# LayerNorm statistics in bf16, V behind Q in the first pair, fewer warm-up matmuls, and b2 added on VectorE, in a one-core transformer block

## The chip, the cores and the metric

The kernel runs on one core of a Trainium2 chip. The metric is the device time of one execution in microseconds; lower is better. The engines are named as in the profile: PE (TensorE matmuls), PEld (its weight loads), DVE (VectorE), ACT (ScalarE), POOL (GpSimd), and SP, which issues the DMAs.

## The reference

One transformer block over x of 1 x 2048 x 1024 in bf16, with 32 heads of 32:

```python
h  = x + (softmax(q k^T / sqrt(32)) v) @ wo       # q, k, v = layernorm(x) @ wqkv, per head
h2 = h + gelu(layernorm(h) @ w1 + b1) @ w2 + b2   # w1 1024 x 3584, gelu by tanh
```

layernorm subtracts the mean and divides by sqrt(variance + 1e-5), with no gain and no offset. All the inputs and the output are bf16.

## The kernel before

**Tiling.** The 2048 rows are 16 tiles of 128 or 8 chunks of 256. The 32 heads are 8 groups g of 4 heads (128 columns). A *round* (`Job.round`) is the scores of one g, one chunk of queries and 256 keys: eight matmuls with K = 32, four side by side in the array (line 705), two Exp of 128 x 1024 on ACT (713), an addition on DVE for the softmax sum (720), eight matmuls of P times V (725), and four with a column of ones for the sum (744). There are 8 x 8 x 8 = 512 rounds, so 1024 Exp. Scores lie in three pairs of PSUM banks and a round uses two pairs, so the scores of a round wait for the first Exp of the round before.

**Stages.** In the *lead*, the x tiles come two by two (eight pairs): LayerNorm on DVE (`layer_norm`), transposition (`tr_tile`, on PE for the first two pairs, by DMA for the others), the projections K, Q and V of the first heads, and the first 16 rounds. The statistics of the second x tile are taken by ACT (554). Then come the other groups' projections with the attention of chunks 0 and 1, and after that, per chunk c, attention(c) with work of the chunks before put between: the output projection `wo(c-1)`, `ln2(c-1)`, `ffn2(c-2)` and `ffn1(c-1)`. In the *tail*, after the last Exp, come wo(7), ln2(7), what is left of ffn2(6), ffn1(7) and ffn2(7). ffn2 of a chunk is four *groups* (two tiles of rows by two halves of the columns) of 28 accumulating matmuls of 512 columns. Ahead of them in a group stands a matmul that puts 2 x b2 into PSUM, from `two_row` (a matrix with 2.0 in row 0) and `b2t` (b2 in row 0, zeros below; 867). DVE then writes 0.5 x PSUM + h (875). The tail's ffn2(7) has no such matmul: there b2 is loaded on all partitions into `b2b` (1025) and added to h in f32 (`hb`, 1027).

**Order.** The program's order on each engine is worked out when the kernel is built. Every piece of work is a task with a cost in microseconds, a priority and dependencies; `Graph.schedule` plays them through, and `pick_pe` chooses PE's next one: scores first when they are ready, then PV, then the *background* (projections, wo, ffn), then warm-up matmuls (`kind="warm"`) if there is nothing else. The costs that matter here are 0.930 and 0.915 for the two Exp of a round (`EXP`, 473), 0.2165 for a 512-column background matmul (`mm`), 0.217 for a round's scores, and 0.108 for a change of PE's tiling mode (`switch`, 112). On the chip each engine then runs its list strictly in that order, with semaphores between engines. Background matmuls go as four column tiles of 32 (502) or, in ffn1, the lead and the tail, as one full matmul (505).

**LayerNorm** (545 to 581): `bn_stats` twice and `bn_aggr` per tile give mean and variance in f32 (`mv`). A copy rounds them to bf16 (`mvb`, 570), an addition puts eps on the variance (571), POOL takes the root (573), a copy turns the mean into f32 (575), and a reciprocal (576) and the normalisation (578) follow.

**Warm-up** (903): 80 matmuls of 256 columns that read `ident` and `b2t`. They wait for POOL's setting of both; the memset of `b2t` is POOL's last (540).

```python
    EXP = (0.930, 0.915)
...
        proj_k(group("lead", FULL), 0, 256 * i, 256, "act")
        if i < 2:
            proj_q(group("lead", FULL), 0, 256 * i, 256, i, "dve")
        proj_v(group("lead", FULL), 2 * i, 0, "act")
```

Of the kernel before, what the change touches and what calls it, by code (L numbers as in the profile page):

```python
# [8 lines left out]
ALU = mybir.AluOpType  # L9
# [3 lines left out]
P = 128  # L13
BF = dt.bfloat16
# [298 lines left out]
def build_kernel(nc, A_x, A_wqkv, A_wo, B_w1, B_b1, B_w2, B_b2, out):  # L313
# [45 lines left out]
    top = Area(BASE)  # L359
    ident, B_ident = sb(top, "ident", [P, P], BF)  # L360
    ones32, B_ones = sb(top, "ones32", [P, 32], BF)
    two_row, B_two = sb(top, "two_row", [P, P], BF)
    b2t, B_b2t = sb(top, "b2t", [P, D], BF)
    b1b, B_b1b = sb(top, "b1b", [FC, P], BF)
    b1f, B_b1f = sb(top, "b1f", [P, FC], F32)
    cexp, B_cexp = sb(top, "cexp", [P, 16], F32)
    NLN = 8
    st_l, B_stl = sb(top, "st", [P, NLN, 12], F32, NLN)
    mv_l, B_mv = sb(top, "mv", [P, NLN, 2], F32, NLN)
    mvb, B_mvb = sb(top, "mvb", [P, NLN, 2], BF, NLN)  # L370
    mvr, B_mvr = sb(top, "mvr", [P, NLN, 1], F32, NLN)
    tb, B_tb = sb(top, "tb", [P, NLN, 1], BF, NLN)
    denb, B_denb = sb(top, "denb", [P, NLN, 1], BF, NLN)
# [106 lines left out]
    def group(name, full=False):  # L480
        g = Group((1, len(groups)), gr.buf())
        g.full = full
        g.name = name
        groups.append(g)
        return g

    def grp_pe(g, fns, occ, reads, mode):
        t = pe(fns, occ, reads=reads, writes=[g.buf], mode=mode)
        t.grp = g
        return t  # L490

# [36 lines left out]
    def dma_t(out_ap, in_ap, reads, writes, prio=0):  # L528
# [3 lines left out]
    pool(lambda g: g.affine_select(out=ident[:], in_=ident[:], compare_op=ALU.not_equal, fill=1.0,  # L532
                                   base=0, pattern=[[-1, P]], channel_multiplier=1), 0.4,
         reads=[B_ident], writes=[B_ident])
    pool(lambda g: g.memset(cexp[:, 0:8], 0.5), 0.2, writes=[B_cexp])
    pool(lambda g: g.memset(cexp[:, 8:16], -1.0), 0.2, reads=[B_cexp], writes=[B_cexp])
    pool(lambda g: g.memset(ones32[:], 1.0), 0.2, writes=[B_ones])
    pool(lambda g: g.memset(two_row[:], 0.0), 0.3, writes=[B_two])
    pool(lambda g: g.memset(two_row[0:1, :], 2.0), 0.3, reads=[B_two], writes=[B_two])
    pool(lambda g: g.memset(b2t[:], 0.0), 1.0, writes=[B_b2t])  # L540

    cnt = {"ln": 0}
    LEAD_PRIO = -4
# [1 line left out]
    def layer_norm(tiles, prio, on_act=(), after=()):  # L545
        n = len(tiles)
        while cnt["ln"] % NLN + n > NLN:
            cnt["ln"] += 1
        i = cnt["ln"] % NLN
        cnt["ln"] += n  # L550
        for k, (x_ap, B_x, o_ap, B_o) in enumerate(tiles):
            if k in on_act:
                for f, fn in enumerate((ACT.Copy, ACT.Square)):
                    act(lambda a, k=k, x_ap=x_ap, f=f, fn=fn: a.activation(
                        junk, x_ap, fn, scale=1.0, accum_out=st_l[:, i + k, f:f + 1]), 1024 + 112,
                        reads=B_x, writes=[B_stl[i + k], B_junk], prio=-1)
                dve(lambda v, k=k: v.tensor_scalar(mv_l[:, i + k, 0:1], st_l[:, i + k, 0:1], 1.0 / D, None, ALU.mult), 0.12,
                    reads=[B_stl[i + k]], writes=[B_mv[i + k]], prio=prio)
                dve(lambda v, k=k: v.scalar_tensor_tensor(st_l[:, i + k, 2:3], mv_l[:, i + k, 0:1], -1.0, mv_l[:, i + k, 0:1], ALU.mult, ALU.mult),
                    0.12, reads=[B_mv[i + k]], writes=[B_stl[i + k]], prio=prio)  # L560
                dve(lambda v, k=k: v.scalar_tensor_tensor(mv_l[:, i + k, 1:2], st_l[:, i + k, 1:2], 1.0 / D, st_l[:, i + k, 2:3], ALU.mult, ALU.add),
                    0.12, reads=[B_stl[i + k]], writes=[B_mv[i + k]], prio=prio)
                continue
            for c in range(2):
                dve(lambda v, c=c, k=k, x_ap=x_ap: v.bn_stats(st_l[:, i + k, 6 * c:6 * c + 6], x_ap[:, 512 * c:512 * c + 512]),
                    0.68, reads=[B_x[c % len(B_x)]], writes=[B_stl[i + k]], prio=prio, after=after)
            dve(lambda v, k=k: v.bn_aggr(mv_l[:, i + k, :], st_l[:, i + k, :]), 0.2,
                reads=[B_stl[i + k]], writes=[B_mv[i + k]], prio=prio)
        sl = slice(i, i + n)
        dve(lambda v: v.tensor_copy(mvb[:, sl, :], mv_l[:, sl, :]), 0.12, reads=B_mv[sl], writes=B_mvb[sl], prio=prio)  # L570
        dve(lambda v: v.tensor_scalar(tb[:, sl, :], mvb[:, sl, 1:2], EPS_BF, None, ALU.add), 0.12,
            reads=B_mvb[sl], writes=B_tb[sl], prio=prio)
        pool(lambda g: g.tensor_tensor(denb[:, sl, 0], tb[:, sl, 0], cexp[:, 0:n], ALU.pow), 0.42 + 0.157 * n,
             reads=B_tb[sl] + [B_cexp], writes=B_denb[sl], prio=prio)
        dve(lambda v: v.tensor_copy(mvr[:, sl, :], mvb[:, sl, 0:1]), 0.12, reads=B_mvb[sl], writes=B_mvr[sl], prio=prio)
        dve(lambda v: v.reciprocal(rden[:, sl, :], denb[:, sl, :]), 0.12, reads=B_denb[sl], writes=B_rden[sl], prio=prio)
        for k, (x_ap, B_x, o_ap, B_o) in enumerate(tiles):
            t = dve(lambda e, k=k, x_ap=x_ap, o_ap=o_ap: e.tensor_scalar(
                o_ap, x_ap, mvr[:, i + k, :], rden[:, i + k, :], ALU.subtract, ALU.mult), 0.58,
                reads=B_x + [B_mvr[i + k], B_rden[i + k]], writes=[B_o], prio=prio)  # L580
        return [t]
# [217 lines left out]
    def ln2_tile(R, c, t, evac):  # L799
        o, bo = R.xb.next()  # L800
        layer_norm([(hch[:, c % 2, t, :], B_hch[c % 2][2 * t:2 * t + 2], o, bo)], LN2_PRIO)
        if evac == "dma":
            dma_t(hnT[:, t, :, :], o, [bo], [B_hnT[t]], prio=-1)
        else:
            transposes(group(f"t{c}.{t}"), o, bo, hnT[:, t, :, :], B_hnT[t], evac)

    def ln2(R, c, evac):
        for t in range(2):
# [46 lines left out]
    def ffn2(R, c, j, t, tail=False):  # L855
# [4 lines left out]
        for h in range(512 // n):  # L860
            grp = group(f"f2.{c}.{j}{t}.{h}")
            grp.soft = {d for _, _, d in ws}
            grp.dmas = [d for _, _, d in ws]
            grp.soft |= soft[c]
            grp.gate = [gate[c]]
            if not tail:
                mm(grp, two_row[:, :], b2t[:, 512 * j:512 * j + 512], True, False, [B_two, B_b2t])
            at = slice(512 * j + n * h, 512 * j + n * h + n)
            for fc in range(FC):
                w, bw, _ = ws[fc // 4]  # L870
                mm(grp, gT[:, c % 2, fc, t * P:t * P + P], w[:, fc % 4, n * h:n * h + n], tail and fc == 0, fc == FC - 1,
                   [B_gT[c % 2][fc], bw], cols=(0, n))
            o, bo = R.os.next()
            h_ap, b_h = (hb[:, t, at], B_hb[t]) if tail else (hch[:, c % 2, t, at], B_hch[c % 2][2 * t + j])
            dve(lambda v, o=o, h_ap=h_ap, grp=grp: v.scalar_tensor_tensor(
                o[:, 0:n], psum[:, grp.bank, 0:n], 0.5, h_ap, ALU.mult, ALU.add),
                c_dve_ps(n), reads=[grp.buf, b_h], writes=[bo], prio=-2)
            dma(out2[256 * c + P * t:256 * c + P * t + P, at], o[:, 0:n], P * n * 2, reads=[bo], prio=0)
# [21 lines left out]
    load_w(WV, -6, 0, 2 * P)  # L900
    for tt in range(4, NXR):
        x_tile(tt, -6)
    for k in range(80):
        pe(lambda p: p.matmul(psum[:, 6, 0:256], ident[:, :], b2t[:, 0:256], start=True, stop=True), 0.12,  # L904
           reads=[B_ident, B_b2t], writes=[B_ps[6]], kind="warm")
# [4 lines left out]
    for i in range(8):  # L910
# [9 lines left out]
                last_x = [x_tile(tt + NXR, -4)]  # L920
        proj_k(group("lead", FULL), 0, 256 * i, 256, "act")
        if i < 2:
            proj_q(group("lead", FULL), 0, 256 * i, 256, i, "dve")
        proj_v(group("lead", FULL), 2 * i, 0, "act")
        jobs[0].round()
        if i == 1:
            jobs[1].round()
# [23 lines left out]
        rest_w(WQ + 1, c * P, c * P + P)  # L951
    rest_w(WV + 1, 256, 512)
    dma(b1b[:], B_b1.rearrange("(fc p) -> fc p", p=P), P * FC * 2, writes=[B_b1b], prio=1, after=lx)
    dma(b2t[0:1, :], B_b2.rearrange("(o d) -> o d", o=1), D * 2, writes=[B_b2t], prio=1, after=lx)

    n_lead = len(groups)
    B_ps[4].r += [t for grp in groups for t in grp.buf.r]
# [52 lines left out]
    hb, B_hb = sb(tail, "hb", [P, 2, D], F32, 2)  # L1010
    b2b, B_b2b = sb(tail, "b2b", [P, D], BF)
    slots = []
    for k in range(7):
        for lo, nm in ((kt_lo, "wk"), (v_lo, "wv")):
# [6 lines left out]
    for t in range(2):  # L1021
        for j in range(2):
            wo_group(R2, L, j, t, ws[j])
        ln2_tile(R2, L, t, "act")
    dma(b2b[:], B_b2.rearrange("(o d) -> o d", o=1).broadcast_to((P, D)), P * D * 2, writes=[B_b2b], prio=1)
    for t in range(2):
        dve(lambda v, t=t: v.tensor_tensor(hb[:, t, :], hch[:, L % 2, t, :], b2b[:], ALU.add), c_dve(1024),
            reads=B_hch[L % 2][2 * t:2 * t + 2] + [B_b2b], writes=[B_hb[t]], prio=2)
# [170 lines left out]
```

## Time and profile before

| | |
|---|---|
| median of 4 runs | 1106.34 us (1104.67 to 1106.88) |
| the profiled execution, its own time | 1106.86 us |
| its span, first to last instruction | 1105.1 us |
| PE busy | 1067.2 us (97%) |
| ACT busy | 1025.7 us (93%) |
| DVE busy | 819.5 us (74%) |
| POOL busy | 19.2 us (2%) |
| first Exp starts, last one ends | 16.19 and 1029.20 us |
| last matmul ends | 1102.49 us |

The busy share of PE comes from records whose ends are modelled and overlap, so it is read with the starts of the instructions beside it. The time of the execution is 1.8 us over its span: launch and end lie around it.

### The profile page before, as it was taken

Reading aid. Unit: us, or ns where it says so; the run is one execution under the profiler, and the core shown is the slowest. Engines: PE = TensorE matmul, PEld = TensorE weight load, DVE = VectorE, ACT = ScalarE, POOL = GpSimd, SP = SyncE. Lnnn points to the kernel's source line nnn. Section 1 sums busy time; section 2 is a strip of 40 time slices with the busy share of each in tenths; the row PEclk is TensorE's granted clock in tenths of the full one; section 3 lists DMA queues with packets and bytes.
Section 4 is the critical chain, followed back from the end, with each engine's and each line's share of the span. In section 5 each row is a group of like instructions: output and inputs, shape, how many; then the busy total and the mean of one; then the engine's idle time right before and its main releaser. Section 6 shows DMA issues by size and latency. Waiting matters only on the chain.

```text
span 1105.1 us, 42019 instructions
## 1 busy us (share of the span) xinstructions
PE 1067.2 (97%) x19196; PEld 595.0 (54%) x19196; DVE 819.5 (74%) x1461; ACT 1025.7 (93%) x1135; POOL 19.2 (2%) x37
## 2 busy tenths in 40 slices
PE   8999999999999989999999999999999999999999
PEld 6645555554444655554554455455545544554585
DVE  7456666666767888888888688878887887787563
ACT  5889999999999999999999999999999999999351
POOL 1100000000000000000000000000000000000000
PEclk9999999999999989999999999999999999999999
DMA  6960100012432854676847755764767377968770
GB/s 190 194 172 2 41 2 3 3 41 88 104 107 88 222 131 126 187 237 141 248 119 245 192 167 174 210 207 124 246 138 245 101 230 195 282 167 266 229 238 20
DMA packets 263164, 169.17 MB, mean 153 GB/s; under 512 B 50763, under 2 KB 260811, under 8 KB 262988
## 3 DMA queue, kind: packets, MB, share of 16 engines
q1 hardware_dynamic: 262988, 166.50, 53.4%
q8 instruction: 150, 2.46, 1.0%
q14 instruction: 26, 0.21, 0.1%
HBM read 152.31 MB, written 7.34 MB: 144 GB/s over the span
## 4 chain that ended last, share of the span: by engine, by line
ACT 55%; PE 43%; DVE 1%; issue 0%; POOL 0%; DVEq 0%; POOLq 0%
ACT PT L713 52%; PE ps L505 16%; PE ps L502 13%; PE ps L705 6%; PE ps L725 4%; ACT a_th L848 3%; PE ps L744 2%; PE ps L904 1%; PE ps L585 0%; DVE stg L598 0%; ACT xnT L588 0%; DVE PS L720 0%; DVE DT L753 0%; ACT V L596 0%; DVE hch L790 0%
## 5 line engine op out<-in xcount | busy, mean ns | idle before, releaser
L713 ACT ACTIVATE PT<-ps 128x1024 bf16<-128x1024 f32 x1024 | 953.8, 1075 | 12.7 <-PE ps L705 11.8
L720 DVE TENSOR_TENSOR PS<-PT 128x1024 bf16<-128x1024 bf16 x495 | 333.3, 685 | 104.3 <-ACT PT L713 80.2
L705 PE MATMUL ps<-QT,KT 32*128 32x256 bf16 x4096 | 204.0, 273 | 12.9 <-ACT PT L713 11.9
L505 PE MATMUL ps<-hnT,w1r 128*128 128x256 bf16 x1632 | 208.9, 275 | 3.9 <-DVE gT L830 1.7
L502 PE MATMUL ps<-w2r,gT 128*32 128x512 bf16 x2860 | 192.9, 383 | 0.1
L725 PE MATMUL ps<-PT,V 128*32 128x256 bf16 x4096 | 184.5, 275 | 8.7 <-ACT PT L713 7.8
L505 PEld LDWEIGHTS ps<-hnT,w1r 128*128 128x128 bf16 x1632 | 146.7, 98 | 57.2 <-issue 31.0
L705 PEld LDWEIGHTS ps<-QT,KT 32*128 32x128 bf16 x4096 | 61.1, 92 | 163.6 <-ACT PT L713 124.5
L744 PE MATMUL ps<-PS,ones 128*32 128x256 bf16 x1980 | 138.5, 275 | 1.5 <-DVE PS L720 1.2
L725 PEld LDWEIGHTS ps<-PT,V 128*32 128x32 bf16 x4096 | 91.9, 96 | 71.7 <-ACT PT L713 30.4
L502 PE MATMUL ps<-xnT,Wall 128*32 128x512 bf16 x1888 | 127.0, 381 | 3.1 <-DVE stg L598 1.3
L502 PEld LDWEIGHTS ps<-w2r,gT 128*32 128x32 bf16 x2860 | 67.2, 97 | 64.9 <-issue 26.1
L830 DVE TENSOR_TENSOR gT<-ps,b1f 128x512 bf16<-128x512 f32 x98 | 67.3, 687 | 21.8 <-PE ps L505 20.8
L505 PE MATMUL ps<-Wall,xnT 128*128 128x128 bf16 (+1 forms) x896 | 69.6, 227 | 0.5 <-DVE V L598 0.3
L502 PEld LDWEIGHTS ps<-xnT,Wall 128*32 128x32 bf16 x1888 | 43.0, 96 | 46.9 <-issue 14.4
L744 PEld LDWEIGHTS ps<-PS,ones 128*32 128x32 bf16 x1980 | 52.4, 96 | 27.1 <-issue 12.1
L849 DVE SCALAR_TENSOR_TENSOR gT<-a_th,gT 128x1024 bf16<-128x1024 f32 x49 | 59.7, 1219 | 5.7 <-ACT a_th L848 5.6
L505 PEld LDWEIGHTS ps<-Wall,xnT 128*128 128x128 bf16 x896 | 54.9, 98 | 15.5 <-issue 11.1
L502 PE MATMUL ps<-w1r,OT 128*32 128x512 bf16 x896 | 62.0, 381 | 1.0 <-DVE hch L790 0.9
L846 DVE SCALAR_TENSOR_TENSOR a_sq<-a_sq,gT 128x1024 bf16<-128x1024 bf16 x49 | 59.8, 1220 | 0.7
L848 ACT ACTIVATE a_th<-a_sq 128x1024 f32<-128x1024 bf16 x49 | 54.9, 1120 | 0.0
L753 DVE STREAM_TRANSPOSE DT<-ps 128x256 f32<-128x256 f32 x64 | 28.6, 446 | 24.1 <-PE ps L744 24.0
(85 smaller groups left out, 589.8 us busy)
## 6 DMA issues: line engine op xcount, KB each, us to landing
w2r<-in_B_w_dram SPq DMA_DIRECT2D x105, 512.0 KB, 6.3
w1r<-in_B_w_dram SPq DMA_DIRECT2D x102, 512.0 KB, 4.6
w1r<-in_A_wo_dram SPq DMA_DIRECT2D x28, 512.0 KB, 3.9
wk<-in_B_w_dram SPq DMA_DIRECT2D x9, 512.0 KB, 6.3
xrb<-in_A_x_dram SPq DMA_DIRECT2D x16, 256.0 KB, 4.4
Wall<-in_A_wqkv_dram SPq DMA_DIRECT2D x16, 256.0 KB, 5.2
wv<-in_B_w_dram SPq DMA_DIRECT2D x8, 512.0 KB, 6.6
a_x<-in_A_x_dram SPq DMA_DIRECT2D x28, 128.0 KB, 2.3
```

The lines of the kernel that those rows point to most:

```text
L502: fns.append(lambda p, j=j: p.matmul(dst(32 * j, 32 * j + 32), lhsT[:, 32 * j:32 * j + 32], rhs, start=start, stop=stop, tile_position=(0, ...
L505: t.alt = [lambda p: p.matmul(dst(0, P), lhsT, rhs, start=start, stop=stop, skip_group_check=True)]
L705: fns.append(lambda p, i=i, hh=hh, r0=r0: p.matmul(psum[:, 2 * us[hh // 2] + hh % 2, 256 * i:256 * i + 256], KT[r0:r0 + 32, g, 256 * r + P ...
L713: t = act(lambda a, u=u, q=q: a.activation(PT[:, s, 2 * q:2 * q + 2, :], psum[:, 2 * u:2 * u + 2, :], ACT.Exp, bias=0.0, scale=SCALE), 102 ...
L720: dve(lambda v: v.tensor_tensor(PS[:, z, :, :], PT[:, s, :, 0:256], PT[:, s, :, 256:512], ALU.add), c_dve(1024, 2), reads=B_PT[s], writes= ...
L725: fns.append(lambda p, i=i, hh=hh: p.matmul(psum[32 * hh:32 * hh + 32, self.bank, 0:256], V[:, g, 2 * r + i, 32 * hh:32 * hh + 32], PT[:, ...
L744: fns.append(lambda p, i=i, hh=hh, src=src: p.matmul(psum[32 * hh:32 * hh + 32, self.bank, 256:512], ones32[:, :], src[:, hh, :], start=False,
L753: dve(lambda v: v.transpose(DT[f][:], psum[:, self.bank, 256:512]), c_dve_ps(256), reads=[self.buf], writes=[B_DT[f]], prio=-1)
L830: gate[c] = dve(lambda v, xh=xh, fc=fc, grp=grp: v.tensor_tensor(xh, psum[:, grp.bank, :].rearrange("p (f n) -> p f n", f=2), b1f[:, fc:fc ...
L846: dve(lambda v: v.scalar_tensor_tensor(v4(sq), v4(sq), C2, xh, ALU.add, ALU.mult), c_dve(n), reads=[b_sq] + b_xh, writes=[b_sq], prio=1)
L848: gate[c] = act(lambda a: a.activation(th, sq, ACT.Tanh, bias=0.0, scale=K2 / 2), n, reads=[b_sq], writes=[b_th], prio=-1, kind="tanh")
L849: t = dve(lambda v: v.scalar_tensor_tensor(xh, v4(th), 1.0, xh, ALU.add, ALU.mult), c_dve(n), reads=[b_th] + b_xh, writes=b_xh, prio=1)
```

## The change

It makes five edits. (1) `bn_aggr` writes mean and variance in bf16, the rounding copy goes, and the copy of the mean to f32 is put before POOL's root; for the tile whose statistics ACT takes, the mean is computed straight in f32. (2) In the first pair, V's matmuls may start only after Q's last. (3) The warm-up is 56 matmuls of 128 columns that read `ident` alone, planned at 0.1 each. (4) The matmul of 2 x b2 goes from every ffn2 group, with `two_row`, `b2t` and their memsets; b2 is loaded on all partitions near the end of the lead, and after each LayerNorm of h an addition on DVE adds it to h in place in bf16, for the tail too, whose f32 copy goes. (5) The planner's cost of the two Exp falls to 0.922 and 0.907.

```diff
-    EXP = (0.930, 0.915)
+    EXP = (0.922, 0.907)
...
-    pool(lambda g: g.memset(two_row[:], 0.0), 0.3, writes=[B_two])
-    pool(lambda g: g.memset(two_row[0:1, :], 2.0), 0.3, reads=[B_two], writes=[B_two])
-    pool(lambda g: g.memset(b2t[:], 0.0), 1.0, writes=[B_b2t])
...
-        dve(lambda v: v.tensor_copy(mvb[:, sl, :], mv_l[:, sl, :]), 0.12, reads=B_mv[sl], writes=B_mvb[sl], prio=prio)
-        dve(lambda v: v.tensor_scalar(tb[:, sl, :], mvb[:, sl, 1:2], EPS_BF, None, ALU.add), 0.12,
-            reads=B_mvb[sl], writes=B_tb[sl], prio=prio)
+        dve(lambda v: v.tensor_scalar(tb[:, sl, :], mv_l[:, sl, 1:2], EPS_BF, None, ALU.add), 0.15,
+            reads=B_mv[sl], writes=B_tb[sl], prio=prio)
+        if not on_act:
+            dve(lambda v: v.tensor_copy(mvr[:, sl, :], mv_l[:, sl, 0:1]), 0.15, reads=B_mv[sl], writes=B_mvr[sl], prio=prio)
...
+        h = hch[:, c % 2, t, :]
+        dve(lambda v: v.tensor_tensor(h, h, b2b[:], ALU.add), c_dve(1024, 2),
+            reads=[B_b2b], writes=B_hch[c % 2][2 * t:2 * t + 2], prio=2)
...
-            if not tail:
-                mm(grp, two_row[:, :], b2t[:, 512 * j:512 * j + 512], True, False, [B_two, B_b2t])
...
-    for k in range(80):
-        pe(lambda p: p.matmul(psum[:, 6, 0:256], ident[:, :], b2t[:, 0:256], start=True, stop=True), 0.12,
-           reads=[B_ident, B_b2t], writes=[B_ps[6]], kind="warm")
+    for k in range(56):
+        pe(lambda p: p.matmul(psum[:, 6, 0:P], ident[:], ident[:], start=True, stop=True), 0.1,
+           reads=[B_ident], writes=[B_ps[6]], kind="warm")
...
-            proj_q(group("lead", FULL), 0, 256 * i, 256, i, "dve")
-        proj_v(group("lead", FULL), 2 * i, 0, "act")
+            q = group("lead", FULL)
+            proj_q(q, 0, 256 * i, 256, i, "dve")
+        v = group("lead", FULL)
+        if i == 0:
+            v.after = q.buf.w
+        proj_v(v, 2 * i, 0, "act")
...
-    dma(b2t[0:1, :], B_b2.rearrange("(o d) -> o d", o=1), D * 2, writes=[B_b2t], prio=1, after=lx)
+    dma(b2b[:], B_b2.rearrange("(o d) -> o d", o=1).broadcast_to((P, D)), P * D * 2, writes=[B_b2b], prio=1, after=lx)
...
-    dma(b2b[:], B_b2.rearrange("(o d) -> o d", o=1).broadcast_to((P, D)), P * D * 2, writes=[B_b2b], prio=1)
-    for t in range(2):
-        dve(lambda v, t=t: v.tensor_tensor(hb[:, t, :], hch[:, L % 2, t, :], b2b[:], ALU.add), c_dve(1024),
-            reads=B_hch[L % 2][2 * t:2 * t + 2] + [B_b2b], writes=[B_hb[t]], prio=2)
```

More of the change, by code (lines that the diff above doesn't have):

```diff
@@ L361, in build_kernel @@
     ones32, B_ones = sb(top, "ones32", [P, 32], BF)
-    two_row, B_two = sb(top, "two_row", [P, P], BF)
-    b2t, B_b2t = sb(top, "b2t", [P, D], BF)
+    b2b, B_b2b = sb(top, "b2b", [P, D], BF)
     b1b, B_b1b = sb(top, "b1b", [FC, P], BF)
     b1f, B_b1f = sb(top, "b1f", [P, FC], F32)
-    cexp, B_cexp = sb(top, "cexp", [P, 16], F32)
+    cexp, B_cexp = sb(top, "cexp", [P, 8], F32)
     NLN = 8
     st_l, B_stl = sb(top, "st", [P, NLN, 12], F32, NLN)
-    mv_l, B_mv = sb(top, "mv", [P, NLN, 2], F32, NLN)
-    mvb, B_mvb = sb(top, "mvb", [P, NLN, 2], BF, NLN)
+    mv_l, B_mv = sb(top, "mv", [P, NLN, 2], BF, NLN)
     mvr, B_mvr = sb(top, "mvr", [P, NLN, 1], F32, NLN)
@@ L482, in group @@
         g.full = full
+        g.after = ()
         g.name = name
@@ L487, in grp_pe @@
     def grp_pe(g, fns, occ, reads, mode):
-        t = pe(fns, occ, reads=reads, writes=[g.buf], mode=mode)
+        t = pe(fns, occ, reads=reads, writes=[g.buf], mode=mode, after=g.after)
         t.grp = g
@@ L534, in build_kernel @@
          reads=[B_ident], writes=[B_ident])
-    pool(lambda g: g.memset(cexp[:, 0:8], 0.5), 0.2, writes=[B_cexp])
-    pool(lambda g: g.memset(cexp[:, 8:16], -1.0), 0.2, reads=[B_cexp], writes=[B_cexp])
+    pool(lambda g: g.memset(cexp[:], 0.5), 0.2, writes=[B_cexp])
     pool(lambda g: g.memset(ones32[:], 1.0), 0.2, writes=[B_ones])
-    pool(lambda g: g.memset(two_row[:], 0.0), 0.3, writes=[B_two])
-    pool(lambda g: g.memset(two_row[0:1, :], 2.0), 0.3, reads=[B_two], writes=[B_two])
-    pool(lambda g: g.memset(b2t[:], 0.0), 1.0, writes=[B_b2t])
     cnt = {"ln": 0}
@@ L556, in layer_norm @@
                         reads=B_x, writes=[B_stl[i + k], B_junk], prio=-1)
[L557 to L560, printed above, removed]
+                dve(lambda v, k=k: v.tensor_scalar(mvr[:, i + k, :], st_l[:, i + k, 0:1], 1.0 / D, None, ALU.mult), 0.12,
+                    reads=[B_stl[i + k]], writes=[B_mvr[i + k]], prio=prio)
+                dve(lambda v, k=k: v.scalar_tensor_tensor(st_l[:, i + k, 2:3], mvr[:, i + k, :], -1.0, mvr[:, i + k, :], ALU.mult, ALU.mult),
+                    0.12, reads=[B_mvr[i + k]], writes=[B_stl[i + k]], prio=prio)
                 dve(lambda v, k=k: v.scalar_tensor_tensor(mv_l[:, i + k, 1:2], st_l[:, i + k, 1:2], 1.0 / D, st_l[:, i + k, 2:3], ALU.mult, ALU.add),
@@ L569, in layer_norm @@
         sl = slice(i, i + n)
-        dve(lambda v: v.tensor_copy(mvb[:, sl, :], mv_l[:, sl, :]), 0.12, reads=B_mv[sl], writes=B_mvb[sl], prio=prio)
-        dve(lambda v: v.tensor_scalar(tb[:, sl, :], mvb[:, sl, 1:2], EPS_BF, None, ALU.add), 0.12,
-            reads=B_mvb[sl], writes=B_tb[sl], prio=prio)
+        dve(lambda v: v.tensor_scalar(tb[:, sl, :], mv_l[:, sl, 1:2], EPS_BF, None, ALU.add), 0.15,
+            reads=B_mv[sl], writes=B_tb[sl], prio=prio)
+        if not on_act:
+            dve(lambda v: v.tensor_copy(mvr[:, sl, :], mv_l[:, sl, 0:1]), 0.15, reads=B_mv[sl], writes=B_mvr[sl], prio=prio)
         pool(lambda g: g.tensor_tensor(denb[:, sl, 0], tb[:, sl, 0], cexp[:, 0:n], ALU.pow), 0.42 + 0.157 * n,
              reads=B_tb[sl] + [B_cexp], writes=B_denb[sl], prio=prio)
-        dve(lambda v: v.tensor_copy(mvr[:, sl, :], mvb[:, sl, 0:1]), 0.12, reads=B_mvb[sl], writes=B_mvr[sl], prio=prio)
-        dve(lambda v: v.reciprocal(rden[:, sl, :], denb[:, sl, :]), 0.12, reads=B_denb[sl], writes=B_rden[sl], prio=prio)
+        dve(lambda v: v.reciprocal(rden[:, sl, :], denb[:, sl, :]), 0.15, reads=B_denb[sl], writes=B_rden[sl], prio=prio)
         for k, (x_ap, B_x, o_ap, B_o) in enumerate(tiles):
@@ L870, in ffn2 @@
                 w, bw, _ = ws[fc // 4]
-                mm(grp, gT[:, c % 2, fc, t * P:t * P + P], w[:, fc % 4, n * h:n * h + n], tail and fc == 0, fc == FC - 1,
+                mm(grp, gT[:, c % 2, fc, t * P:t * P + P], w[:, fc % 4, n * h:n * h + n], fc == 0, fc == FC - 1,
                    [B_gT[c % 2][fc], bw], cols=(0, n))
             o, bo = R.os.next()
-            h_ap, b_h = (hb[:, t, at], B_hb[t]) if tail else (hch[:, c % 2, t, at], B_hch[c % 2][2 * t + j])
+            h_ap, b_h = hch[:, c % 2, t, at], B_hch[c % 2][2 * t + j]
             dve(lambda v, o=o, h_ap=h_ap, grp=grp: v.scalar_tensor_tensor(
@@ L1009, in build_kernel @@
     R2.os = Ring(ring(tail, "b_os", 3, 512, BF))
-    hb, B_hb = sb(tail, "hb", [P, 2, D], F32, 2)
-    b2b, B_b2b = sb(tail, "b2b", [P, D], BF)
     slots = []
```

## The prediction

> **What bounds it now.** I read the busy shares first, then the chain that ended last, then the groups by form, then windows and timeline of the stages that the change touches.
>
> ```profile
> PE 1067.2 (97%) x19196; PEld 595.0 (54%) x19196; DVE 819.5 (74%) x1461; ACT 1025.7 (93%) x1135; POOL 19.2 (2%) x37
> ACT 55%; PE 43%; DVE 1%; issue 0%; POOL 0%; DVEq 0%; POOLq 0%
> ```
>
> The chain is shared by ACT and PE, and nothing else is on it. The windows tell the stages apart (columns: length; busy us and count of PE, PEld, DVE, ACT, POOL; granted clock; DMA share; GB/s):
>
> ```profile
> 430.00:1000.00 570.00, 555.14 (x10364) 299.92 (x10360) 462.27 (x790) 568.87 (x618) 6.44 (x10) 1.00 0.66 191
> 1030.30:1102.50 72.20, 72.19 (x487) 46.23 (x483) 37.21 (x54) 20.46 (x37) 1.10 (x2) 1.00 0.56 175
> ```
>
> The second line is the tail: PE without a gap, so what it has left to do there is its length. The first is attention with background. ACT is full, but is it the bound? In the timeline's start column the second Exp of a round starts 0.904 or 0.921 us after the first (mean 0.911), while the next round's first starts on average 0.935 later, 0.904 in six cases of ten. A round therefore takes 1.846 us (570 us less 40 tanh of 0.947, over 577 Exp, gives 1.844); the planner assumed 0.930 + 0.915 = 1.845. ACT alone could do 2 x 0.904 = 1.81. On PE, scores that follow ffn or wo matmuls start a median 0.105 us after these stream out; any change of tiling mode costs that much, so PE usually comes straight from other work. So PE's list, packed to 1.845, sets the pace, and ACT's waits (0.037 a round) are too short for the table of waits. **PE is the bound from about 56 us to 1102.5**, with ACT 2% behind.
>
> **b2 on DVE.** 7 chunks x 4 groups = 28 matmuls of 2 x b2 go. The groups by form show 104 records in four column tiles (26 groups) and 2 full ones:
>
> ```profile
> L502 PE MATMUL ps<-b2t,two_row 128*32 128x512 bf16 x104 | 10.4, 388 | 0.4 <-DVE hch L790 0.3
> L505 PE MATMUL ps<-b2t,two_row 128*128 128x512 bf16 x2 | 0.8, 379 | 0.0
> L720 DVE TENSOR_TENSOR PS<-PT 128x1024 bf16<-128x1024 bf16 x495 | 333.3, 685 | 104.3 <-ACT PT L713 80.2
> L1027 DVE TENSOR_TENSOR hb<-hch,b2b 128x1024 f32<-128x1024 bf16 x2 | 2.4, 1220 | 0.0
> ```
>
> The 388 ns is one record's length, not what PE pays, since four run side by side and the next is pipelined behind. What it pays is start to start:
>
> ```profile
> 429.12 0.40 PE L502 MATMUL ps<-b2t,two_row 128*32 128x512 bf16 x4
> 429.34 1.90 PE L502 MATMUL ps<-w2r,gT 128*32 128x512 bf16 x32
> ```
>
> 0.22 here, 0.2157 as a mean over neighbours of the same form. 28 x 0.2157 = **6.0 us off PE**: 5.6 during attention (429 to 1025 us), 0.43 in the tail. No mode change goes with it. The 5.6 count only if the freed slots fill. ffn2(6) runs ahead into attention: one group of it and 15 of 28 blocks of the next are done before the tail. So work moves up from the tail.
>
> DVE gets 16 additions of 0.685 (L720's form) and loses two of 1.22. The two tail ones have PE's unbroken 72 us over them. The 14 in attention (9.6 us) lie in DVE's idle 108 of 570 us. Queued behind one on DVE are PSUM evacuations and L720's sums, for which PE waits; the lowest priority puts it where the plan has a hole. Cost 0; if that cover were gone, each would hold PE up by its length, 9.6 us. The 256 KB load of b2b is issued where the row of b2t was (67.0 us), behind the weights of wqkv and ahead of w2 blocks that land every 1.5 us (512 KB), so it pushes these back by 0.75; w2 is first used at 429. Nothing else is moved on SP, and the same load at 1028.5 goes.
>
> **The start.** From the timeline:
>
> ```profile
> 2.65 5.66 PE L904 MATMUL ps<-b2t,ident 128*128 128x256 bf16 x33 [2.65 <-POOL b2t L540]
> 5.22 0.17 DVE L570 CAST mvb<-mv 128x2 bf16<-128x2 f32 x1
> 5.42 0.16 DVE L571 TENSOR_SCALAR tb<-mvb 128x1 bf16<-128x1 bf16 x1
> ...
> 8.15 0.61 PE L585 MATMUL ps<-ident,xb 128*128 128x128 bf16 x8
> ...
> 10.45 0.61 PE L585 MATMUL ps<-ident,xb 128*128 128x128 bf16 x8
> ...
> 12.27 1.03 PE L505 MATMUL ps<-xnT,Wall 128*128 128x256 bf16 x8
> 13.13 0.82 PE L505 MATMUL ps<-Wall,xnT 128*128 128x256 bf16 x6
> 13.86 1.03 PE L505 MATMUL ps<-xnT,Wall 128*128 128x256 bf16 x8
> ```
>
> A removed copy takes 0.20 (5.22 to 5.42) out of each of the first two LayerNorms, in series: the second tile's output ends at 8.87 instead of 9.27 (8.72 + 0.55). The f32 copy of the mean ends before POOL's root does (5.64 against 6.23): nothing. The transposes could have started at 7.05 and 9.3, but began at 8.04 and 10.34 (weight loads), behind warm-ups. After, POOL has set ident at 1.45, so warming starts about 1.5; in the planner's own costs 56 x 0.1 fit ahead of the first transposes (before, 33 x 0.12 stood there, from plan time 3.0; now it starts at 0.8), so the list has all 56 first and none later. In time, 56 of half the length end near 7.1. The second transposes then start at 8.9, 1.5 before 10.45, and K with them (its weights landed at 5.7, Q's at 6.7). Six V matmuls go from between K and Q: 0.73. The first scores wait for Q's copy: 1.5 + 0.7 = **2.3 earlier** at best. The lead then loops through ACT, PE and ACT at 5.3 us a pair and should carry it; LayerNorm of the second pair, which stood behind Q's copy on DVE (to 15.28), moves too.
>
> Against it: **the clock**. Warm-ups started 0.213 apart until 6.5 us and 0.109 after, half and full speed. Now PE is sparse from 7.1 to 10.8. The windows show that sparseness alone halves the clock:
>
> ```profile
> 23.60:27.02 3.42, 1.95 (x33) 1.00 0.94 223
> 402.48:405.90 3.42, 1.04 (x28) 1.00 0.71 175
> 405.90:409.31 3.41, 3.00 (x45) 0.50 0.65 84
> 1010.06:1013.47 3.41, 2.02 (x48) 1.00 1.17 315
> 1013.47:1016.88 3.41, 3.41 (x36) 0.50 0.95 296
> ```
>
> (columns: length, PE busy, clock, DMA). Its steps fall on one grid of 3.41 us. By streaming time (256 columns in 0.109, side by side counted once) PE was used 18% and 37% ahead of the two falls, and 42% in 23.6 to 27.0, with no fall. The new start has 20 to 45% in such a stretch, by where the grid falls: about an even chance. Half speed for K and Q's 16 matmuls costs 16 x 0.104 = 1.7, leaving 0.6; two slow windows (3.4 lost) would leave a loss of 1.1. I take 1.5 earlier, between 0.6 and 2.3. *TensorE: Matmul & The Clock Gate* of the Trainium skill, in "Why this matters for your kernels", says that pauses up to about 3 us between bursts keep the clock. By it the start gains the whole 2.3. The fall at 1013 came with no pause of 1 us, so the row decides, and I keep 1.5.
>
> **The Exp cost.** 0.016 less a round changes only the order: less background between scores. 498 rounds follow the lead, so 8.0 us of background moves toward the tail. If PE sets the pace, rounds shorten by the same and nothing is lost (perhaps ACT's 0.037 waits shrink: a gain of up to 2). If ACT does, all 8.0 is added. The nearest row, 1.846 measured against 1.845 planned, says the first; since ACT's floor is close I take a fifth, +1.6.
>
> **Other.** 23 copies of DVE off the start's path go, 0.2 each, under waits; layout shifts by some 320 bytes: 0.
>
> **Sum**, from the profiled 1106.86 (span 1105.1 + 1.8; 0.5 above the median): - 6.0 - 1.5 + 1.6 = **1100.9**.
>
> **Rivals.** (a) *The start loses*: two slow windows, 1106.9 - 6.0 + 1.1 + 1.6 = 1103.5. (b) *The removal frees nothing*: background waits for something else, as at 399 to 409 (ffn1's one input buffer) and 1009 to 1013 (the last gelu); only the tail's 0.43 is left: 1106.9 - 0.4 - 1.5 + 1.6 = 1106.5. Against: such stretches are rare from 429 on. (c) *Exp, the slower side*: the rounds stay at 1.846 and all 8.0 lands in the tail: 1106.9 - 6.0 - 1.5 + 8.0 = 1107.3. It decides once over 7.5 of the 8.0 is not won back, a round above 1.845. For: ACT is 99.8% busy. Against: its starts. (d) *DVE holds PE*: + 9.6, 1110.5; against: 81% busy. (e) *Better*: Exp costs nothing, the start gains 2.3, one slow window (1.7) goes: 1106.9 - 6.0 - 2.3 - 1.7 = 1096.8.
>
> **Chances.** Forecast 0.55, (a) 0.12, (b) 0.08, (c) 0.07, (d) 0.05, (e) 0.13. 0.2% is about what this measurement can tell. Faster by more (under 1104.1): forecast, (a), (e): 0.80. Within: (b) and half of (c): 0.12. Slower: the rest, 0.08. The range leaves out (c), (d) and half of (e): 1096.8 to 1106.5.
>
> **What would show it.** First Exp at 13.9 to 15.6 instead of 16.19; K's eight matmuls 0.109 apart (0.213 if the clock fell); rounds near 1.83 and the last Exp 7 or more earlier; from the last Exp to the last matmul 72 to 77 against 73.3; no waits of PE on the additions. Wrong if rounds stay at 1.845 with a longer tail, or if a new stretch without background appears near chunk boundaries: the order is planned anew everywhere.

## The result and the profile after

The changed kernel takes **1103.48 us** (median of 44 runs, 1100.83 to 1107.03) where the kernel before, on the same chips, takes 1106.77 (65 runs, 1104.0 to 1109.36): a ratio of **0.997, 95% interval 0.9965 to 0.9976**, or 3.3 us less. The forecast was 6.0 less. The sign and the range held; about half of the forecast gain is missing, and the rest of this document is about where it went.

The profiled execution took 1104.98 us, with a span of 1103.2. It is 1.9 below the one before. Runs of one kernel vary with their mean clock, so the medians differ by more than the two profiles: of the 44, the nine at 0.995 have a median of 1101.9, the seventeen at 0.992, the profiled one among them, 1104.0. Lines in the profile after are numbered a little differently: scores 700, Exp 708, sums 715, PV 720, background matmuls 501 and 504, tanh 846, the new addition 802.

Busy shares and the engines of the chain that ended last, in the page of the changed kernel:

```profile
PE 1059.5 (96%) x19045; PEld 588.6 (53%) x19045; DVE 824.0 (75%) x1449; ACT 1022.5 (93%) x1135; POOL 20.3 (2%) x33
ACT 77%; PE 20%; DVE 1%; DMA 1%; issue 0%; POOL 0%; DVEq 0%; POOLq 0%
```

PE is busy 7.7 us less. The chain is a first hint: ACT's share went from 55% to 77%, PE's from 43% to 20%. Work was taken from PE, and the end is now tied to ACT much more.

The windows of the changed kernel (length; busy us and count of PE, PEld, DVE, ACT, POOL; granted clock; DMA share; GB/s), for a piece of the start, for attention with background, and for the tail:

```profile
11.78:15.19 3.41, 3.41 (x18) 2.31 (x16) 2.06 (x7) 0.38 (x1) 0.70 (x1) 0.50 0.46 167
...
430.00:1000.00 570.00, 555.40 (x10326) 299.64 (x10329) 471.55 (x795) 568.21 (x619) 8.42 (x10) 1.00 0.68 194
...
1027.29:1100.68 73.39, 73.35 (x492) 46.69 (x488) 36.16 (x52) 20.46 (x37) 1.54 (x2) 1.00 0.57 177
```

The first line is a stretch at half clock that the start did not have before. The second looks like the old one (555.14 PE, 568.87 ACT), but one tanh more fits in beside the same 577 Exp: a round takes 1.840 us instead of 1.846, worked out from the starts of the Exp as in the prediction. The third shows the tail: the last Exp ends at 1026.50 (2.7 earlier) and the last matmul at 1100.68 (1.8 earlier), so the tail is 74.2 instead of 73.3.

The start on PE, from the timeline of the changed kernel (start, us, engine, line, operation, tiles, count, and in brackets the idle time before it and what ended it):

```profile
1.53 4.86 PE L900 MATMUL ps<-ident 128*128 128x128 bf16 x55 [1.53 <-POOL ident L531]
7.06 0.62 PE L580 MATMUL ps<-ident,xb 128*128 128x128 bf16 x8 [0.67 <-DVE mvr L552]
7.52 0.22 PE L900 MATMUL ps<-ident 128*128 128x128 bf16 x1
9.21 0.61 PE L580 MATMUL ps<-ident,xb 128*128 128x128 bf16 x8 [1.47 <-DVE xb L573]
10.93 2.82 PE L504 MATMUL ps<-xnT,Wall 128*128 128x256 bf16 x16 [1.12 <-ACT xnT L583]
13.54 1.85 PE L504 MATMUL ps<-Wall,xnT 128*128 128x256 bf16 x8
15.32 0.40 PE L700 MATMUL ps<-QT,KT 32*128 32x256 bf16 x8
```

Warm-ups start at 1.53 and the transpositions at 7.06 and 9.21 (forecast 7.05 and 8.9). But K and Q's 16 matmuls take 2.82, and V's eight take 1.85 where six took 0.82 before: the clock fell. The first Exp starts at 15.77, only 0.4 earlier than before.

### The profile page after: what moved, and what is told of

It is laid out like the page before. It is cut to its first block, busy times and chain, and to the rows that moved or that the text cites. A ratio compares the mean times of both kernels' runs of the same rounds, so it can differ in the third digit from the quotient of the medians.

```text
span 1103.2 us, 41713 instructions
## 1 busy us (share of the span) xinstructions
PE 1059.5 (96%) x19045; PEld 588.6 (53%) x19045; DVE 824.0 (75%) x1449; ACT 1022.5 (93%) x1135; POOL 20.3 (2%) x33
## 4 chain that ended last, share of the span: by engine, by line
ACT 77%; PE 20%; DVE 1%; DMA 1%; issue 0%; POOL 0%; DVEq 0%; POOLq 0%
ACT PT L708 73%; PE ps L504 10%; PE ps L501 5%; ACT a_th L846 4%; PE ps L700 2%; PE ps L720 2%; PE ps L739 1%; DMA hnT<-xb 1%; ACT xnT L583 0%; DMA xrb<-in_A_x_dram 0%; DVE xb L573 0%; DVE stg L593 0%; PE ps L580 0%; DVE st L560 0%; DVE a_os L871 0%
## 5 line engine op out<-in xcount | busy, mean ns | idle before, releaser
L708 ACT ACTIVATE PT<-ps 128x1024 bf16<-128x1024 f32 x1024 | 952.4, 1107 | 16.3 <-PE ps L700 15.7
```

What stands on the lines that cost most here:

```text
L708: t = act(lambda a, u=u, q=q: a.activation(PT[:, s, 2 * q:2 * q + 2, :], psum[:, 2 * u:2 * u + 2, :], ACT.Exp, bias=0.0, scale=SCALE), 102 ...
```

## The experiments

Two theories. **Terms:** each edit has its own price (PE work saved, start, Exp costs), and the prices add up; one of them was mis-sized. **Order:** PE is not the bound alone, so PE time saved or added counts only partly, and what decides is whether PE has background ready; the edits need not add up, since each one makes the planner lay out all lists anew. A special case of the second is the **gelu gate**: ffn2 of a chunk may start only after the chunk's last tanh, and the VectorE steps of gelu have a low priority (1, behind LayerNorm's -2 and the sums' -1) on an engine that runs its list strictly in order. (Letters in the quoted expectations are explained in each.)

All twelve runs; each ratio is to the kernel before on the same chip, so runs are compared by their ratios. "Rounds" is the mean length of a round from 430 to 1000 us; the tail runs from the end of the last Exp to the end of the last matmul; the "gate" columns are the start of the last tanh of the fifth and of the seventh chunk; "dry" is the sum of all stretches over 2.6 us after 430 in which PE has attention but no background matmul; "half clock" is the time at 0.50 after 430.

| kernel | median us | ratio [95%] | rounds | last Exp ends | tail | gate 5 | gate 7 | dry | half clock |
|---|---|---|---|---|---|---|---|---|---|
| before | 1106.77 | 1 | 1.846 | 1029.2 | 73.3 | 805.9 | 1012.4 | 10.4 | 3.4 |
| after | 1103.48 | 0.997 [0.9965, 0.9976] | 1.840 | 1026.5 | 74.2 | 815.1 | 1012.3 | 13.3 | 3.4 |
| b2 edit alone | 1118.75 | 1.0115 [1.0099, 1.0132] | 1.854 | 1028.9 | 83.9 | 822.3 | 1029.0 | 27.2 | 23.9 |
| Exp edit alone | 1116.98 | 1.0097 [1.0082, 1.0112] | 1.841 | 1022.6 | 89.0 | 829.7 | 1036.4 | 7.9 | 13.6 |
| start edits alone | 1107.93 | 1.0017 [1.0008, 1.0026] | 1.842 | 1024.8 | 77.7 | 819.2 | 1016.2 | 8.2 | 3.4 |
| before, b2 matmuls not issued | 1107.14 | 0.9999 [0.9987, 1.0010] | 1.847 | 1029.6 | 73.2 | 805.4 | 1013.1 | 10.7 | 3.4 |
| after, 28 matmuls doubled | 1106.3 | 0.9994 [0.9984, 1.0005] | 1.849 | 1025.3 | 74.9 | 816.3 | 1012.1 | 12.7 | 0 |
| after, additions cut short | 1102.55 | 0.9962 [0.9947, 0.9977] | 1.837 | 1024.2 | 74.0 | 814.9 | 1011.2 | 13.0 | 0 |
| after, 130 warm-ups | 1102.3 | 0.9971 [0.9958, 0.9985] | 1.839 | 1023.8 | 74.2 | 814.1 | 1010.6 | 12.8 | 0 |
| b2 edit, gelu first | 1107.82 | 1.0008 [0.9998, 1.0018] | 1.850 | 1027.9 | 74.9 | 800.0 | 1015.2 | 12.6 | 3.4 |
| before, gelu first | 1107.91 | 1.0007 [0.9996, 1.0019] | 1.847 | 1025.7 | 75.6 | 808.1 | 1014.6 | 8.2 | 0 |
| Exp edit, last gelu first | 1109.89 | 1.0026 [1.0016, 1.0037] | 1.843 | 1024.3 | 79.9 | 806.8 | 1020.5 | 17.5 | 10.2 |
| after, old Exp costs | 1105.56 | 0.9987 [0.9976, 0.9998] | 1.847 | 1030.2 | 72.2 | 805.6 | 1013.7 | 17.6 | 3.4 |
| after, 130 warm-ups, Exp 0.913 | 1107.1 | 1.0009 [0.9998, 1.0021] | 1.836 | 1020.8 | 82.1 | 830.5 | 1021.6 | 14.5 | 0 |

Rounds, gates, dry, half clock and the ends are of one profiled execution each, the medians of all runs.

### One part at a time

The b2 edit alone, on the kernel before (with `b2b` loaded in place of `b2t` and the tail's copy gone):

```diff
-            if not tail:
-                mm(grp, two_row[:, :], b2t[:, 512 * j:512 * j + 512], True, False, [B_two, B_b2t])
+        h = hch[:, c % 2, t, :]
+        dve(lambda v: v.tensor_tensor(h, h, b2b[:], ALU.add), c_dve(1024, 2), ...
```

> The kernel before with edit (4) alone: no matmul of 2 x b2, b2 added to h on VectorE; warm-ups, LayerNorm, V's place and the Exp cost stay. Theory (PE sets the pace, so freed slots fill): 6.0 us faster than before, with the last Exp about where it was and the tail shorter. Rival (the freed slots stay empty): 0.4 faster. Rival (VectorE's 14 additions hold PE up): no gain or slower.

Measured: 1118.75, **12.4 slower** than the 1106.35 of the kernel before.

The Exp edit alone:

```diff
-    EXP = (0.930, 0.915)
+    EXP = (0.922, 0.907)
```

> The kernel before with edit (5) alone: planned Exp costs 0.922 and 0.907. Theory (PE sets the pace): rounds about 0.012 us shorter, tail longer by nearly as much, time 0 to 1.6 us over before. Rival (ACT sets the pace): rounds stay at 1.846 and the time rises by up to 8 us.

Measured: 1116.98, **10.6 slower**. The last Exp does end 6.6 earlier, but the tail is 15.7 longer.

The start edits alone (bf16 statistics, V behind Q, 56 warm-ups):

```diff
-    for k in range(80):
+    for k in range(56):
...
+        if i == 0:
+            v.after = q.buf.w
```

> The kernel before with edits (1) to (3) alone: statistics in bf16, V behind Q, 56 short warm-ups. The matmuls of 2 x b2 stay. Theory: first Exp 0.4 to 2.3 us earlier and the time 0.6 to 2.3 lower. Rival (the clock falls at 11.8 us, as in the profile after, and the lead's second round comes no earlier than before): 0 to 1 us slower.

Measured: 1107.93, 1.6 slower, although the first Exp started at 14.07 in the profile, 2.1 earlier. The last Exp came 4.4 earlier there, but the tail is 4.4 longer.

Alone the three cost 12.4 + 10.6 + 1.6 = 24.6; together they gain 3.3. The theory of terms in its plain form is gone: no sum of fixed prices gives both.

### What stands in the b2 edit's way

The trace of the b2 edit alone shows a long dry stretch. PE's ffn2, wo and other four-tile matmuls (line 502), in windows of 12.8, 12.4 and 12.8 us (length; PE and PEld busy; clock; DMA share; GB/s):

```profile
795.00:807.80 12.80, 8.61 (x128) 2.81 (x120) 1.00 0.57 153
807.80:820.20 12.40, 0.04 (x4) 0.00 (x0) 0.65 0.73 128
820.20:833.00 12.80, 5.48 (x88) 1.98 (x88) 0.80 0.23 69
```

For 12.4 us there is none but the last four records of a group at the edge (and none of line 505 either), and the clock halves. Why, its timeline tells, first on VectorE, then on ACT:

```profile
802.66 1.22 DVE L849 SCALAR_TENSOR_TENSOR a_sq<-a_sq,gT 128x1024 bf16<-128x1024 bf16 x1
...
805.39 0.69 DVE L565 BATCH_NORM_STATS2 st<-hch 128x6 f32<-128x512 bf16 x1
...
808.74 0.69 DVE L565 BATCH_NORM_STATS2 st<-hch 128x6 f32<-128x512 bf16 x1
...
815.85 0.55 DVE L578 TENSOR_SCALAR xb<-hch,mvr,rden 128x1024 bf16<-128x1024 bf16 x1 [1.24 <-DMA hnT<-xb]
...
816.92 1.22 DVE L852 SCALAR_TENSOR_TENSOR gT<-a_th,gT 128x1024 bf16<-128x1024 f32 x1
...
818.66 0.69 DVE L848 TENSOR_TENSOR a_sq<-gT 128x1024 bf16<-128x1024 bf16 x1
...
820.03 1.22 DVE L849 SCALAR_TENSOR_TENSOR a_sq<-a_sq,gT 128x1024 bf16<-128x1024 bf16 x1
...
804.49 1.15 ACT L851 ACTIVATE a_th<-a_sq 128x1024 f32<-128x1024 bf16 x1
822.33 1.05 ACT L851 ACTIVATE a_th<-a_sq 128x1024 f32<-128x1024 bf16 x1
```

The sixth tanh of the chunk ends at 805.6. Its last VectorE step (852) comes only at 816.92, because both LayerNorms of the next chunk (565 to 578), with attention's sums between, stand ahead of it in VectorE's list, and the second of them waits 1.24 us for the transposing DMA to free its buffer. The seventh and last gelu follows after that, its tanh at 822.33, and ffn2 of that chunk starts at 826.7. In the kernel before the same tanh started at 805.93 and ffn2 at 813.5:

```profile
805.93 1.12 ACT L848 ACTIVATE a_th<-a_sq 128x1024 f32<-128x1024 bf16 x1
```

That the gate costs time, and how much, was then tried by moving gelu ahead in the planner:

```diff
-        dve(lambda v: v.tensor_tensor(v4(sq), xh, xh, ALU.mult), c_dve(n, 2), reads=b_xh, writes=[b_sq], prio=1)
+        dve(lambda v: v.tensor_tensor(v4(sq), xh, xh, ALU.mult), c_dve(n, 2), reads=b_xh, writes=[b_sq], prio=-1)
```

(and the same for its two other VectorE operations), on the b2 edit alone:

> b2_only (edit 4 alone, 12 us slower than before) with the planner's priority of gelu's three operations on VectorE raised from 1 to -1, so that they go ahead of the softmax sums and of other work that is not in a hurry. Theory: b2_only lost its time where the last tanh of a chunk came late (822 and 1029 us, 12 and 11 us of PE without background), since gelu's VectorE work stood behind LayerNorm and sums. Then the last tanh of chunks 4 and 6 comes by about 806 and 1018, the stretch at 808 without background is gone, and the kernel is 5 to 8 us faster than b2_only, at 1111 to 1114. Rival (the stretches come from the weights' DMAs or from the 14 additions): they stay and the time is that of b2_only.

Measured: 1107.82, 0.9 over the 1106.97 of the kernel before on its chip, so 11.5 of the 12.4 us are back, more than the 5 to 8 expected. Its timeline, VectorE and then ACT:

```profile
797.50 0.69 DVE L849 TENSOR_TENSOR a_sq<-gT 128x1024 bf16<-128x1024 bf16 x1
798.23 1.22 DVE L850 SCALAR_TENSOR_TENSOR a_sq<-a_sq,gT 128x1024 bf16<-128x1024 bf16 x1
...
800.68 0.69 DVE L565 BATCH_NORM_STATS2 st<-hch 128x6 f32<-128x512 bf16 x1
...
799.99 1.07 ACT L852 ACTIVATE a_th<-a_sq 128x1024 f32<-128x1024 bf16 x1
```

The last gelu now goes ahead of LayerNorm, its tanh at 799.99 instead of 822.33. The same edit on the kernel before is the control:

> The kernel before with gelu's three VectorE operations ahead of their place (planner priority -1 instead of 1) and nothing else. It recovered 11 us in the kernel with b2 on VectorE. Theory A (that kernel's gelu happened to be stuck, before's is not): no more than 2 either way, 1105 to 1109. Rival (gelu ahead is a gain of its own, whatever the order): 1096 to 1102.

Measured: 1107.91, ratio 1.0007 [0.9996, 1.0019]: nothing gained where gelu was not stuck. So the 11.5 us are not a general gain of that priority. How much of them is the wait for gelu and how much the half clock that comes with it (23.9 us at half clock in the b2 edit alone, 3.4 here) no run separates.

For the Exp edit alone, only the last gelu of each chunk was moved ahead:

```diff
+        pr = 1 if fc + nf < FC else -3
-        dve(... reads=b_xh, writes=[b_sq], prio=1)
+        dve(... reads=b_xh, writes=[b_sq], prio=pr)
```

> The kernel before with the Exp costs of the change (0.922, 0.907) alone, and of gelu only the last step of each chunk put ahead on VectorE (planner priority -3 instead of 1 for its three operations). The Exp costs alone gave 1116.98 with the last tanh of the fifth chunk at 829.7 us and of the seventh at 1036.4. Theory A (the 10 us are gelu's last step stuck behind LayerNorm2 on VectorE, and the gate of ffn2 with it): those tanh start by 815 and 1018, the tail falls from 89 to 74 to 80, time 1104 to 1110. Theory B (the 10 us are the 8.0 us of background that cheaper Exp moves to the tail, with nothing won back): the tail stays at 85 or more, 1113 to 1117.

Measured: 1109.89, 3.0 over the 1106.93 of the kernel before on its chip, so 7.7 of 10.6 us are back. The fifth chunk's tanh starts at 806.8 instead of 829.7, the seventh's at 1020.5 (2.5 later than expected), the tail is 79.9. The sixth chunk's is as late as ever, 929.4 instead of 930.3, with a dry stretch of 10.6 us from 918.6 and a half clock of 10.2 from 924. The rest of the loss may lie there; that was not tried by itself. The three kernels that lost most (b2 alone, Exp alone, this one) are the three with over 10 us at half clock after 430.

### What 28 matmuls are worth when the order stays

Here each list stays as it was planned, and only what is issued differs. On the order of before, the 28 b2 matmuls are planned but not issued; b2 is left out of the first seven chunks:

```diff
+    for t in b2mm:
+        t.fns = []
```

> The kernel before with its order of instructions kept and the 28 matmuls of 2 x b2 not issued, so b2 is left out for the first seven chunks. If PE sets the pace: 3 to 6 us faster than before. If ACT does, or the slots stay empty: 0.4 to 1.

Measured: 0.9999 [0.9987, 1.0010], so **0.1 us, within 1.4, for 6.0 us of PE work taken away**. On the order of after, the first matmul of each of 28 groups is issued twice:

```diff
+    for t in twice:
+        t.fns = t.fns + t.fns
```

> The changed kernel with its order of instructions kept, and the first matmul of each of the 28 ffn2 groups ahead of the tail issued twice (the result stays the same). It asks what such a matmul costs when nothing is planned anew. If PE sets the pace: 28 x 0.2157 = 6.0 us over the changed kernel. If the slots were idle anyway: 0.4 (the two in the tail) to 1.5.

Measured: 0.9994 [0.9984, 1.0005] against after's 0.997: +2.6 us, within some 1.3, with rounds at 1.849 instead of 1.840. Adding 6.0 us of PE work costs 2.6 of it; taking it away brings nothing that these runs can tell. The windows of the two, on the order of before and of after (555.14 and 555.40 us of PE busy as they were):

```profile
430.00:1000.00 570.00, 552.35 (x10256) 295.92 (x10252) 462.00 (x789) 567.03 (x617) 5.94 (x10) 1.00 0.67 191
...
430.00:1000.00 570.00, 557.29 (x10392) 302.05 (x10392) 469.56 (x792) 568.87 (x617) 8.35 (x10) 1.00 0.66 193
```

The additions of b2, cut to one column of 1024 in after's own order (b2 is left out but for that column):

```diff
-        h = hch[:, c % 2, t, :]
-        dve(lambda v: v.tensor_tensor(h, h, b2b[:], ALU.add), c_dve(1024, 2),
+        h = hch[:, c % 2, t, 0:1]
+        dve(lambda v: v.tensor_tensor(h, h, b2b[:, 0:1], ALU.add), c_dve(1024, 2),
```

> The changed kernel with its order kept and the 16 additions of b2 to h cut to one column of 1024, so that b2 is left out but for that column; each takes about 0.1 us instead of 0.69. If the additions lie in VectorE's idle time: the time of the changed kernel. If they hold PE up: up to 9 us faster than it.

Measured: 0.9962 [0.9947, 0.9977], whose interval overlaps after's: at most some 2.5 us, and not told apart from 0.

### The start and the clock

After, with 130 instead of 56 warm-ups (they are issued only where the planned list has nothing else):

> The changed kernel with 130 warm-up matmuls of 128 columns instead of 56, so that they also fill PE's idle time between the transposes and the first projections. If the half clock between 11.8 and 15.2 us is what ate the start's gain: no half clock there, first Exp near 14 us, and 1.5 to 2.3 us faster than the changed kernel (5 to 6 faster than before). Rival (the lead's later pairs, not the clock, hold the start back): the second pair's first Exp stays near 22.9 and the time is that of the changed kernel.

Measured: 0.9971 [0.9958, 0.9985], the same as after. The profile has no half clock at the start and its first Exp starts at 13.93, as hoped, but the 33rd starts at 64.3, next to 64.5 before: this list is another one, and most of the 2.3 us is lost again between the 7th and the 9th Exp (25.2 to 29.8 where the kernel before takes 27.6 to 30.4).

### The Exp costs

After with the old costs back:

```diff
-    EXP = (0.922, 0.907)
+    EXP = (0.930, 0.915)
```

> The kernel after with the old Exp costs (0.930, 0.915): the Exp edit undone. If the Exp edit has a price of its own of +1.6 (the prediction's term), this runs 1.6 faster than after, 1101.9. If it is nothing by itself: 1103.5 within 1. If the order that is planned decides (a theory without a fixed price per edit), anything from 1101 to 1112, and the sign goes with the start of the last tanh of the fifth and seventh chunk: faster than after only if the seventh's starts before 1012, slower if it starts after 1016.

Measured: 1105.56, ratio 0.9987 [0.9976, 0.9998] beside after's 0.9970: the Exp edit, with the others in place, **gains 1.9 us** (0.0017 of 1106.8; the intervals touch at one end). The seventh tanh starts at 1013.7, between the two conditions set, so the gate does not decide this one. The windows do, for this kernel: the whole middle, and one dry stretch in it:

```profile
499.50:504.00 4.50, 3.25 (x96) 1.75 (x92) 4.37 (x7) 4.50 (x6) 0.00 (x0) 1.00 0.96 275
...
430.00:1000.00 570.00, 551.16 (x10233) 299.78 (x10228) 466.49 (x791) 568.06 (x617) 8.10 (x10) 1.00 0.66 192
```

Between 430 and 1000 the kernel before issues 23 b2 matmuls, 23 x 0.2157 = 5.0 us. Without them, and with rounds as long as before (1.847), PE is busy 551.16 instead of 555.14, 4.0 less, and the tail is only 1.1 shorter (72.2 instead of 73.3), 0.4 of it the two matmuls of its own: **most of the time freed stays empty.** How much exactly the busy column does not tell: with the frozen order, where nothing can move into the slots, it falls by 2.8 only. The timeline shows such a hole:

```profile
499.30 0.61 PE L720 MATMUL ps<-PT,V 128*32 128x256 bf16 x16
...
501.77 0.40 PE L700 MATMUL ps<-QT,KT 32*128 32x256 bf16 x8 [0.33 <-ACT PT L708]
502.68 0.40 PE L720 MATMUL ps<-PT,V 128*32 128x256 bf16 x8 [0.52 <-ACT PT L708]
...
503.60 0.40 PE L700 MATMUL ps<-QT,KT 32*128 32x256 bf16 x8 [0.41 <-ACT PT L708]
503.93 0.83 PE L501 MATMUL ps<-w1r,OT 128*32 128x512 bf16 x12
```

ffn1 of the chunk before ended at 494.7 instead of 496.2, the output projections for which data are there follow, and from 499.5 PE has no background and waits for ACT's Exp (0.33, 0.52 and 0.41 us): by the code the next projections need attention's output, and ffn2 needs the gate (505.2).

Last, in the other direction, a try for a version that beats both: after with 130 warm-ups and still cheaper Exp:

```diff
-    EXP = (0.922, 0.907)
+    EXP = (0.913, 0.898)
-    for k in range(56):
+    for k in range(130):
```

> A try for a version that beats both: the kernel after with 130 instead of 56 warm-up matmuls (1102.3 by itself) and Exp costs 0.913 and 0.898. Scores are issued closer together in the plan, some 9 us more of background moves behind the last Exp. If rounds follow the plan (PE sets the pace): rounds near 1.825, last Exp 7 to 9 earlier than 1023.8, tail 81 to 84, time 1099 to 1103. If ACT's own pace (2 x 0.904 and its waits) now sets the rounds at 1.835 or more: the last Exp only 2 to 3 earlier and the tail 8 longer, 1106 to 1109.

Measured: 1107.1, the second of the two cases. Its windows:

```profile
430.00:1000.00 570.00, 554.76 (x10252) 296.05 (x10244) 467.52 (x789) 569.40 (x621) 6.22 (x10) 1.00 0.66 191
1020.79:1102.86 82.07, 81.46 (x538) 50.63 (x544) 38.27 (x55) 21.52 (x39) 1.54 (x2) 1.00 0.52 164
```

The planner laid a round out at 1.811; it takes 1.836, ACT is busy 569.40 of 570, and the tail is 82.07. The last Exp came 3.0 earlier than with 0.922 and 0.907, the tail is 7.9 longer. No version among those tried beats the changed kernel by more than the runs can tell.

## Why the prediction was right in sign and half in size

- **What bounds it: the step that failed.** "PE is the bound ..., with ACT 2% behind" made 2% into a margin. It is none. With the order frozen, PE relieved of 6.0 us gains 0.1 (within 1.4), and PE given 6.0 us more loses 2.6 (within 1.3). PE and ACT hold each other up: PE's rounds wait for Exp, and its background waits for attention's output and for gelu. A length of 1.846 against a planned 1.845 was read as "PE's list sets the pace". It shows that the plan was met, not that PE had no room.
- **b2 on DVE: -6.0 forecast.** The sum on PE is right (start to start, 28 times). The condition written beside it, "the 5.6 count only if the freed slots fill", is what failed: in the kernel with old Exp costs most of the slots stayed empty (PE 4.0 us less busy, the tail 1.1 shorter). That kernel holds the b2 and start edits, for which -6.0 - 1.5 = -7.5 was forecast; it measured -1.4 (0.9987). This is rival (b), to which 0.08 was given, and its reason against ("such stretches are rare from 429 on") looked only at the old order.
- **DVE's additions: 0.** Held: the short additions are not told apart (0.9962 and 0.997, overlapping).
- **The Exp cost: +1.6 forecast, about -1.9 measured with the other edits in place.** Rounds shortened by 5.6 ns of the planned 16 (498 rounds: 2.8 us), not by nearly all. "Rounds near 1.83 and the last Exp 7 or more earlier" is wrong: 1.840 and 2.7. What rescued the term is the empty slots: they took the background that denser scores pushed aside, so the tail grew by 0.9 and not by 8. That is an inference from the windows of after and of after with old costs (555.40 and 551.16 us busy), and it fits the Exp edit alone, which had no freed slots and whose tail grew by 15.7; there the late gates took their part too.
- **The start: -1.5 forecast.** The mechanism was right, the prices were too favourable by 0.4 to 1.0, and the chance was put into the sum as a mean. Five profiles have the same list for the lead, and the place of the 3.41 us grid made them differ. The 33rd Exp starts at 64.5 in the kernel before; at 63.0 and 63.2 with no half-clock stretch (28 matmuls doubled; start edits alone), at 64.9 with one (after), at 66.0 and 66.1 with two (additions cut short; old Exp costs): -1.5 and -1.3, +0.4, +1.5 and +1.6, where -2.3, -0.6 and +1.1 were forecast for the start. Over such runs the start gains about nothing.
- **The tail: 72 to 77 forecast, 74.2 measured.** Right, but from two errors that cancel: less background pushed back, and less moved up.
- **"Wrong if a new stretch without background appears near chunk boundaries"** was the right place to look. It can have a price of over 10 us, as the b2 edit alone shows, where the rivals stopped at 1110.5; short stretches need not: after with old Exp costs has 17.6 us of them, none over 4.5, and is 1.4 faster than before. That the full change missed it (its seventh gate is at 1012.3, as before) was not foreseeable from the trace of before, and nothing in the prediction earned it: that was luck.
- **The sums** are cut off at the first decimal, not rounded (1100.96 stands as 1100.9, 1103.56 as 1103.5); nothing depends on it.

In the profiles the difference adds up as: start +0.1 (101st Exp at 127.1 instead of 127.0), rounds -2.8, tail +0.9, together the last matmul's -1.8; the profiled execution took 1.9 less.

**What stays open:** why the five edits together leave the seventh gate where it was and the fifth 9 us later without a loss, while single ones shift both by up to 24 us. It is an outcome of list scheduling, and no run shows a rule for it. The gates were moved by a priority, which plans the rest anew as well, so 11.5 and 7.7 us are what those plans are worth, not a clean price of the gate.

## What to carry to other kernels

Before counting work taken off the engine that looks full, ask what the freed slots will run: if the next work there waits for the other full engine, the slots stay empty, and a frozen order with the work left out tells that in one run. Where a planner writes the order, an edit alone says little about that edit: look in its trace for stretches where the filler work runs dry, and at which in-order list its gate is stuck. With two full engines the relief on the one and the denser pace on the other can pay only together: here the relief (with the start edits) gained 1.4, the denser pace alone lost 10.6, and all together gained 3.3.

## What the runs showed of the hardware

The clock can halve without a long pause. It steps on a fixed grid of 3.413 us, and what counts is the used share of one such stretch (by streaming time, as in the prediction): in the starts with the same list of instructions, a stretch used 0.37 (after, 8.37 to 11.78, no pause over 1.47 us) or 0.33 and 0.35 (additions cut short, 6.95 to 10.36 and 17.19 to 20.60) was followed by one at half clock, and one used 0.43 (28 matmuls doubled, 6.27 to 9.69) was not. Worked out in the same way for all 4431 stretches of the fourteen profiles that begin at full clock after 6 us: each of the 26 used up to 0.352 was followed by half clock, three of the seven from 0.365 to 0.378 were, and none of the others was. The rule of pauses up to 3 us, which the prediction cites and sets aside, would have kept the clock in these starts. The grid stands elsewhere in each execution (1.54, 0.12 and 2.86 us after the first instruction in after, additions cut short and 28 matmuls doubled), so the same list meets no, one or two half-clock stretches at its start by chance, worth 3 us between the best and the worst here. *TensorE: Matmul & The Clock Gate* of the Trainium skill, in Part 1, says that the window runs freely and does not reset with the kernel; these traces agree.
